# Shorter idle matmuls in the lead-in, and one unit's block sum rows written later: sparse attention followed by a gated feed-forward

## The chip, the core and the metric

The kernel runs on one core of one Trainium2 chip. The core has a matrix engine (TensorE, PE in the profile, with its weight loads as PEld), VectorE (DVE), ScalarE (ACT), GpSimd (POOL) and a queue engine, SyncE (SP), that here only issues transfers. Transfers are issued from two queues: GpSimd's (they cast from 32 to 16 bits on the way) and SyncE's. Sixteen DMA engines carry both. The metric is the device time of one execution in microseconds; lower is better.

## The reference

The input q, k, v are of shape (4, 8, 768, 64): four units of the batch, eight heads, 768 tokens, 64 numbers. A query sees the keys within 15 tokens of its own, and one summary for each block of 32 tokens (the maximum of its keys, the mean of its values). Then a feed-forward with a gate follows on all 3072 tokens.

```python
k_sum = k.reshape(B, H, nb, block, D).max(axis=3)      # block = 32, nb = 24
v_sum = v.reshape(B, H, nb, block, D).mean(axis=3)
scores_l = scale * np.matmul(q, k.transpose(0, 1, 3, 2))
mask_l = np.abs(pos[:, None] - pos[None, :]) < window   # window = 16
scores_s = scale * np.einsum('bhsd,bhnd->bhsn', q, k_sum) + np.log(block)
...
a = softmax of [scores_l where mask_l, scores_s]
attn = np.matmul(a, np.concatenate([v, v_sum], axis=2))
...
h = x @ w_in                                            # 512 -> 2048
g = h * (1.0 / (1.0 + np.exp(-1.702 * h)))
out = g @ w_out                                         # 2048 -> 512
```

## The kernel before

The four units run one after the other, and each in two halves of 384 tokens. While TensorE computes the feed-forward of one half, the attention of the next is spread between its products. Nearly all engine instructions go through one recording helper (`_Ordered`), which keeps them in the order of the program text on each engine; so all have line 28 in the profile, and tiles tell them apart.

**Lead-in (lines 870 to 980).** The first half of the first unit (the code's unit 0; the change's short description calls the half that follows it "unit 1") is computed on its own, as its data come in. GpSimd issues, in this order: k of the first unit (`load_k0`), q of its first half (`load_q0`), its v (`load_v0`), all of w_in in five parts (`load_w_in`), the first quarter of w_out, the "late q" (q of the second half, `load_q1`, three transfers of 128 tokens for all heads into `qb`), the other quarters of w_out, and then k, q and v of the next batch entry. TensorE has nothing to do until the first k lands; `idle` (line 283) gives it matmuls on a tile of zeros, `warm`, whose results nobody reads. They write the tile ps_h. The first block of them stands at line 902, ahead of the first k turn (`k_turn(0)`, transposes of kb into ps_k).

**The second half's values.** For the second half, `values` multiplies the exponentiated scores with rows of `vw[0]`, a tile in which each 64-query tile has its own 128 rows: 64 rows of v, then the halo of neighbouring v rows, then 24 block sums. Its own rows and the ones column are written by VectorE. The rest is the work of `vrows0` (line 317):

- four copies on VectorE from `vs4` (the sums, in four groups of partitions) to `vs` (32 rows);
- `halo_dmas`: four transfers on SP's queue within `vw[0]`, of 16 partitions each;
- `sum_dmas`: two transfers on SP's queue, 99 KB each, which write the rows of `vs` into `vw[0]`, once for each parity of the query tiles.

`vrows0` is called at line 994, right behind the two copies of v rows into `vw[0]`, while TensorE runs the first half's feed-forward input (`ff_in`, tiles `ph`). After it VectorE builds the second half's keys (tile `kx`). The tile `vs4` lies in the pool `lead`, which `early.close()` (line 1061) gives back; the tiles of the pool `snap`, above all `gs`, take its place in memory, and are first written in the next unit.

**The loop around the change (lines 1066 to 1072).** TensorE computes the first half's output product in twelve slots (`ff_out`, four products of 128x512 each into `po`), and `beside0` puts the second half's attention behind a slot, by this plan:

```python
plan0 = {1: ["q0", "q1", "q2"], 2: ["q3", "s0", "s1"], 4: ["s2", "s3"], 6: ["v0", "v1"], 8: ["x0"], 9: ["x1"]}
```

"q" is `q_late` (line 402): three transposes of the late q on TensorE into ps_q, then a copy on VectorE into qT. "s" is `scores` for one pair of heads (twelve products; exponent on ScalarE) and `mask` on VectorE; "v" is `values` for two pairs (the tile ps_av, 24 products each) and the division by their sums; "x" is the transposition of the result. The PSUM pool behind q0, q1, q3 and the scores has two buffers, taken in turn, so that the second score tile (s1) uses the bank that q3's copy reads. In the built program the first two weight loads and the second product of `v0` hold all the waits for the halo and row transfers.

Of the kernel before, what the change touches and what calls it, by code (L numbers as in the profile page):

```python
# [11 lines left out]
F16 = mybir.dt.float16  # L12
# [23 lines left out]
def kernel(  # L36
# [22 lines left out]
    NT = d_ff // 128  # L59
    HALF = S // 2  # L60
# [18 lines left out]
    early = ExitStack()  # L79
# [203 lines left out]
    def idle(n, cols=128):  # L283

        for i in range(n):
            pe.matmul(out=st["H", 0][:, 0:cols], lhsT=warm[:, 0:128], rhs=warm[:, 0:cols],
                      start=True, stop=True)
# [11 lines left out]
    def halo_dmas(w5, j0):  # L299
        halo_odd(w5, j0)  # L300
        halo_even(w5, j0)
# [10 lines left out]
    def sum_dmas(w5, j0, eng=sp):  # L312
        rows = vs[0:block].unsqueeze(1).to_broadcast([block, NJ - j0, H, VC])
        eng.dma_start(out=w5[64:64 + block, j0:NJ, 0], in_=rows)
        eng.dma_start(out=w5[0:block, j0:NJ, 1], in_=rows)

    def vrows0():

        v6 = vs4.rearrange("p (a g) c -> p g a c", g=4)
        o6 = vs.rearrange("p (a g) c -> p g a c", g=4)  # L320
        for g in range(4):
            dve.tensor_copy(out=o6[0:nb, g, :, 0:D], in_=v6[32 * g:32 * g + nb, g, :, 0:D])
        w5 = vw[0].rearrange("p (j e) h c -> p j e h c", e=2)
        halo_dmas(w5, JH)
        sum_dmas(w5, JH)
# [39 lines left out]
    def k_turn(p):  # L365
        ps = st["K", p] = pturn.tile([128, 1024], BF16, name="ps_k", tag="turn")
        o = 2 * (p % 2)
        for e in range(2):
            turn_plain(ps[:, e * HALF:e * HALF + HALF], kb2[p // 2][:, o:o + 2, e])
# [32 lines left out]
    def q_late(p, eng):  # L402
        if p != 2:
            ps = psb.tile([128, 2048], BF16, name="ps_q", tag="big")
        else:
            ps = pmm.tile([128, 1024], BF16, name="ps_q", tag="mm")
        turn_tiles(ps, qb2["late"][:, :, p], JH)
        copy(eng, qT[p][0][:, HALF:S], ps[:, 0:HALF])
# [163 lines left out]
    def scores(b, half, p):  # L572
        a = a_sb[half, p] = attp.tile([128, 2, TH, QT], BF16, name="a_sb", tag="a_sb")
        big = psb.tile([128, 1024], F32, name="ps_s", tag="big")
        score_tiles(big, p, b % 2, half)
        act.activation(out=a.rearrange("p h t c -> p h (t c)"),
                       in_=big.rearrange("p (h c) -> p h c", h=2)[:, :, 0:HALF],
                       func=ACT.Exp, scale=scale)

    def mask(half, p):  # L580
        a = a_sb[half, p]
        dve.tensor_mul(a, a, mk[:, half * TH:(half + 1) * TH, :].unsqueeze(1)
                       .to_broadcast([128, 2, TH, QT]))

    def values(b, half, g):

        if b == 1:
            banks = [pmm.tile([128, 512], F32, name="ps_av", tag="mm") for i in range(2)]
        else:
            ps = psb.tile([128, 1024], F32, name="ps_av", tag="big")  # L590
            banks = [ps[:, i * 512:i * 512 + 512] for i in range(2)]
        pvs = []
        for i in range(2):
            p = 2 * g + i
            a = a_sb[half, p]
            pv = banks[i][:, 0:390].rearrange("p (h j c) -> p h j c", h=2, j=JH)
            pvs.append(pv)
            for hh in range(2):
                for j in range(JH):
                    for e in range(2):  # L600
                        t = 2 * j + e
                        pe.matmul(out=pv[e * 64:e * 64 + 64, hh, j, :], lhsT=a[:, hh, t, :],
                                  rhs=vw[b % 2][:, half * TH + t, p + hh * NP if b else 2 * p + hh, 0:D + 1],
                                  start=True, stop=True, skip_group_check=True)
        x2[g] = attp.tile([128, 2, JH, 2, D], F16, name="x2", tag="x2", bufs=4)
        for i in range(2):
            norm(x2[g][:, :, :, i].rearrange("p h j d -> p j h d") if b else x2[g][:, i], pvs[i])
# [7 lines left out]
    def tx(half, g):  # L615
        ps = psb.tile([128, 2, HALF], F16, name="ps_x", tag="big")
        for i in range(2):
            for j in range(JH):
                pe.transpose(out=ps[:, i, j * 128:(j + 1) * 128],
                             in_=x2[g][:, i, j].rearrange("p h d -> p (h d)"), identity=ident16)  # L620
        dve.tensor_copy(out=xTT[half][g], in_=ps)
# [17 lines left out]
    def ff_in(half, nts):  # L639

        phs = [pmm.tile([128, HALF], F32, name="ph", tag="mm") for nt in nts]
        for part in ((0, 1), (2, 3)):
            for nt, ph in zip(nts, phs):
                ff_step(ph, half, nt, part)
        for nt, ph in zip(nts, phs):
            gelu(half, nt, ph)
# [31 lines left out]
    def w_sum(what, part):  # L678

        n = NT // 2  # L680
        c = slice(part * n // 2, (part + 1) * n // 2)
        w1, w2 = w_out_sb[:, 0:n], w_out_sb[:, n:]
        b11, b12, b21, b22 = w1[:, c, 0:N1], w1[:, c, N1:], w2[:, c, 0:N1], w2[:, c, N1:]
        a, b = {0: (b12, b11), 1: (b22, ws[:, 0, c]), 2: (b22, b12), 3: (b21, ws[:, 1, c])}[what]
        dve.tensor_tensor(out=ws[:, what, c], in0=a, in1=b, op=ALU.subtract)
# [161 lines left out]
    def ff_out(u, ms, part):  # L847
        if part == 0:
            po_now[ms] = pmm.tile([128, d_model], F32, name="po", tag="mm")
        po = po_now[ms]  # L850
        for nt in range(4 * part, 4 * part + 4):
            pe.matmul(out=po, lhsT=gT[u % 2][:, nt, ms * 128:(ms + 1) * 128],
                      rhs=w_out_sb[:, nt, :], start=(nt == 0), stop=(nt == NT - 1))
        if part == 3:
            osb = outp.tile([128, d_model], F32, name="osb", tag="osb")
            act.activation(out=osb, in_=po, func=ACT.Copy)
            r0 = u * HALF + ms * 128
            sp.dma_start(out=out[r0:r0 + 128, :], in_=osb)
# [5 lines left out]
    def gelu_soon():  # L864

        act.activation(out=gate[:, 1:2], in_=gate[:, 0:1], func=ACT.Gelu_apprx_sigmoid)
# [32 lines left out]
    dve.tensor_copy(out=ident16, in_=ident)  # L899

    st["H", 0] = pturn.tile([128, 512], F32, name="ps_h", tag="turn")
    idle(10, 512)
    k_turn(0)
    k_own(0, act)
    s_bias(0)
# [84 lines left out]
    for e in range(2):  # L990
        r = slice(64 * e, 64 * e + 64)
        dve.tensor_copy(out=w50[r, JH - e:NJ, e, :, 0:D],
                        in_=v0n[r, :, JH - e:NJ, 0:D].rearrange("p h j d -> p j h d"))
    vrows0()
    for s in range(2):
        clear_keys(dve, s)
    for p in range(NP):
# [18 lines left out]
    def beside0(slot):  # L1016
        for what in plan0.get(slot, ()):
            i = int(what[1])
            if what[0] == "q":
                q_late(i, dve)  # L1020
            elif what[0] == "s":
                scores(0, 1, i)
                mask(1, i)
                if i == NP - 1:
                    gelu_soon()
            elif what[0] == "v":
                values(0, 1, i)
            else:
                tx(1, i)
# [28 lines left out]

    for nt in range(N0, NT):
        ff_in(0, (nt,))  # L1060
    early.close()
    snap = ctx.enter_context(tc.tile_pool(name="snap", bufs=1))
    gs = snap.tile([128, 4, NT // 2, HALF], F16, name="gs")
    ws = keep.tile([128, 4, NT // 2, N1], F16, name="ws")
    exp_soon()
    beside0(-1)
    for i, (ms, part) in enumerate((ms, part) for part in range(4) for ms in range(JH)):
        ff_out(0, ms, part)
        beside0(i)
        if i in (10, 11):  # L1070
            w_sum(i - 10, 0)
            w_sum(i - 10, 1)
# [22 lines left out]
    for b in range(1, B - 1):  # L1095
# [32 lines left out]
        i = 0  # L1128
# [98 lines left out]
```

## Time and profile before

| | us |
|---|---|
| median of three timed runs | 209.07 |
| lowest, highest | 208.94, 209.77 |
| the profiled execution, its own time | 208.27 |
| its span, first to last instruction | 206.6 |

The profile shows one execution. The page's first part gives the busy time of each engine, in us and as a share of the span; VectorE is busy for 139.0 us, ScalarE for 123.5. The chain of waits goes back from the last instruction to what released it, step by step, so that the sum of its pieces is the span; pieces named PE are products, named DMA are transfers from issue to landing, "issue" is time in which the engine waited for nothing that the profile shows. In the timeline a row is a start, a length, an engine, the operation with its output and input tiles, and in brackets the idle time ahead of it with what ended it. An entry under SPq or POOL named DMA_DIRECT2D is the issue alone; when the data land is told by the view of a tile.

The page's second part, the span in 40 slices of 5.2 us, gives for TensorE

```profile
PE   7898997999999999999999999999999999999993
DMA  5999999999999999999999999995022940000222
```

where a digit is the busy share in tenths: TensorE has idle time in the first seven slices and the last one, and the DMA engines are occupied there from the second slice on, up to about 145 us.

### The profile page before, as it was taken

To read this page: it belongs to the slowest core of one execution; us is meant where nothing else is said; L and a number is where in the kernel's file an instruction comes from. 1 tells how busy PE (TensorE), PEld (TensorE's weight loads), DVE (VectorE), ACT (ScalarE), POOL (GpSimd) and SP (SyncE) were. 2 spreads that over 40 slices of the span, in tenths; PEclk is the share of its full clock that TensorE was granted. 3 is DMA by queue.
4 is the path that set the end of the run, shared out by engine and by line. 5 is a ranking of instruction groups with operands and counts; after the bars stand their busy time and mean duration, and the time that the engine had idled before them with its cause. 6 is when DMAs were issued, how large, how long until landed. Compare 5 with 4: busy or idle time off the path is not lost.

```text
span 206.6 us, 5777 instructions
## 1 busy us (share of the span) xinstructions
PE 198.3 (96%) x2326; PEld 135.6 (66%) x2326; DVE 139.0 (67%) x387; ACT 123.5 (60%) x236; POOL 93.7 (45%) x144
## 2 busy tenths in 40 slices
PE   7898997999999999999999999999999999999993
PEld 2566553466665566666788876566888865668882
DVE  4766892484965693899667779896769536758221
ACT  2374974637886736677773347778680567984220
POOL 7986588436899585000896017000000009991000
PEclk9999999999999999999999999999999999999999
DMA  5999999999999999999999999995022940000222
GB/s 57 154 159 201 203 197 211 197 157 210 153 148 136 182 174 162 113 172 153 118 160 183 198 115 138 189 223 126 3 105 57 175 127 0 3 0 0 105 102 103
DMA packets 99162, 27.73 MB, mean 134 GB/s; under 512 B 88752, under 2 KB 96192, under 8 KB 99136
## 3 DMA queue, kind: packets, MB, share of 16 engines
q0 software_dynamic: 73504, 13.64, 85.1%
q1 hardware_dynamic: 25632, 13.74, 33.2%
q8 instruction: 18, 0.29, 0.6%
q14 instruction: 8, 0.07, 0.1%
HBM read 27.26 MB, written 6.29 MB: 162 GB/s over the span
## 4 chain that ended last, share of the span: by engine, by line
PE 81%; DMA 12%; POOL 4%; issue 1%; DVE 0%; ACT 0%; POOLq 0%; DVEq 0%
PE ph L28 28%; PE poA L28 16%; PE po L28 10%; PE poB L28 8%; DMA qb<-in_q_dram 8%; DMA w_in_sb<-in_moe_w_in_dram 4%; PE poC L28 4%; PE phA L28 4%; PE ps_s L28 3%; PE ps_av L28 3%; POOL v0n L28 2%; POOL kb L28 1%; PE ps_t L28 1%; PE ps_x L28 1%; PE phB L28 1%; PE phC L28 1%
## 5 line engine op out<-in xcount | busy, mean ns | idle before, releaser
L28 PE MATMUL ph<-xT,w_in_sb 128*128 128x384 f16 x416 | 70.2, 326 | 0.1
L28 PEld LDWEIGHTS <-w_in_sb 128*128 128x128 f16 x452 | 43.7, 98 | 27.8 <-issue 0.2
L28 ACT ACTIVATE gT<-ph 128x384 f16<-128x384 f32 x104 | 49.8, 491 | 18.6 <-PE ph L28 18.3
L28 PEld LDWEIGHTS <-gT 128*128 128x128 f16 x312 | 28.9, 98 | 11.0
L28 ACT ACTIVATE a_sb<-ps_s 128x768 bf16<-128x768 f32 (+1 forms) x32 | 25.0, 826 | 13.8 <-PE ps_s L28 13.8
L28 PEld LDWEIGHTS <-gs 128*128 128x128 f16 x288 | 27.7, 98 | 3.4
L28 POOL DMA_DIRECT2D vw<-in_v_dram x36 | 24.6, 707 | 11.3 <-DMA kb<-in_k_dram 5.0
L28 POOL TENSOR_TENSOR gs<-gT 128x384 f16<-128x384 f16 x9 | 8.2, 910 | 42.4 <-ACT gT L28 42.4
L28 PE MATMUL po<-w_out_sb,gT 128*128 128x512 f16 x96 | 23.6, 380 | 0.0
L28 DVE TENSOR_TENSOR a_sb<-a_sb,mk 128x768 bf16<-128x768 bf16 x28 | 14.8, 554 | 6.5 <-ACT a_sb L28 5.9
L28 PE MATMUL poA<-ws,gs 128*128 128x256 f16 x144 | 18.7, 273 | 0.0
L28 DVE TENSOR_TENSOR x<-ps_av,rc 128x384 f16<-128x384 f32 x32 | 17.8, 557 | 1.1
L28 DVE TENSOR_TENSOR gs<-gT 128x384 f16<-128x384 f16 (+1 forms) x34 | 13.4, 393 | 7.2 <-ACT gT L28 6.9
L28 POOL DMA_DIRECT2D qb<-in_q_dram x17 | 16.4, 983 | 3.2 <-DMA v0n<-in_v_dram 1.1
L28 POOL DMA_DIRECT2D kb<-in_k_dram x16 | 15.3, 972 | 1.8 <-POOLq L1211 0.8
L28 PEld LDWEIGHTS <-kx 64*128 64x128 bf16 (+1 forms) x372 | 9.4, 95 | 6.6 <-issue 4.2
L28 DVE TENSOR_REDUCE ks<-kx 128x24 bf16<-128x768 bf16 x12 | 11.4, 948 | 3.4 <-ACT kx L28 3.2
L28 ACT ACT_TABLE_LOAD x10 | 12.8, 1283 | 1.0 <-PEq L1211 0.8
L28 ACT ACTIVATE osb<-poA 128x256 f32<-128x256 f32 x9 | 3.4, 383 | 15.8 <-PE poA L28 15.8
L28 ACT ACTIVATE s<-poA 128x256 f32<-128x256 f32 x11 | 4.2, 385 | 11.2 <-PE poA L28 11.2
L28 PEld LDWEIGHTS <-a_sb 128*64 128x64 bf16 (+2 forms) x400 | 7.9, 108 | 3.7 <-issue 2.2
L28 PE MATMUL poA<-w_out_sb,gT 128*128 128x256 f16 x72 | 9.4, 273 | 0.0
(112 smaller groups left out, 278.2 us busy)
## 6 DMA issues: line engine op xcount, KB each, us to landing
out_dram<-osb SPq DMA_DIRECT2D x23, 256.0 KB, 3.9
kb<-in_k_dram POOLq DMA_DIRECT2D x16, 192.0 KB, 6.3
qb<-in_q_dram POOLq DMA_DIRECT2D x14, 192.0 KB, 7.9
vw<-in_v_dram POOLq DMA_DIRECT2D x36, 64.0 KB, 5.4
w_out_sb<-in_moe_w_out_dram POOLq DMA_DIRECT2D x4, 512.0 KB, 16.3
w_in_sb<-in_moe_w_in_dram POOLq DMA_DIRECT2D x3, 512.0 KB, 12.6
vw<-vs SPq DMA_DIRECT2D x6, 198.0 KB, 5.6
v0n<-in_v_dram POOLq DMA_DIRECT2D x4, 192.0 KB, 7.8
```

The lines of the kernel that those rows point to most:

```text
L28: r = f(*a, **kw)
```

## The change

Three edits. The first idle block has 36 matmuls of 128 columns (the default of `idle`) instead of ten of 512. The call of `vrows0` moves from line 994 into the loop over the slots, behind `beside0(1)`: in program order that is after the copies of q0, q1 and q2 and before the copy of q3 on VectorE, and ahead of any later entry of SP's queue. And the end of the pool `lead`, with the two lines that open `snap` in its place, moves behind it, since `vrows0` reads `vs4`.

```diff
     st["H", 0] = pturn.tile([128, 512], F32, name="ps_h", tag="turn")
-    idle(10, 512)
+    idle(36)
     k_turn(0)
...
         dve.tensor_copy(out=w50[r, JH - e:NJ, e, :, 0:D],
                         in_=v0n[r, :, JH - e:NJ, 0:D].rearrange("p h j d -> p j h d"))
-    vrows0()
     for s in range(2):
         clear_keys(dve, s)
...
     for nt in range(N0, NT):
         ff_in(0, (nt,))
-    early.close()
-    snap = ctx.enter_context(tc.tile_pool(name="snap", bufs=1))
-    gs = snap.tile([128, 4, NT // 2, HALF], F16, name="gs")
     ws = keep.tile([128, 4, NT // 2, N1], F16, name="ws")
     exp_soon()
     beside0(-1)
     for i, (ms, part) in enumerate((ms, part) for part in range(4) for ms in range(JH)):
         ff_out(0, ms, part)
         beside0(i)
+        if i == 1:
+            vrows0()
+            early.close()
+            snap = ctx.enter_context(tc.tile_pool(name="snap", bufs=1))
+            gs = snap.tile([128, 4, NT // 2, HALF], F16, name="gs")
         if i in (10, 11):
             w_sum(i - 10, 0)
             w_sum(i - 10, 1)
```

In the built program SP's queue has the same order of transfers as before. The four halo transfers wait for the same VectorE instructions as before (the copies of v rows), the two transfers of `sum_dmas` for the copies into `vs` at their new place.

## The prediction

> **What bounds the kernel now.** I read the page's busy shares first, then the chain of waits in order of time, then the timeline of single engines around the two places that the change touches, and last the landing times of the transfers there.
>
> The page says that TensorE is busy nearly all the time, and the chain that the rest is its wait for transfers at the front:
>
> ```profile
> PE 198.3 (96%) x2326; PEld 135.6 (66%) x2326; DVE 139.0 (67%) x387; ACT 123.5 (60%) x236; POOL 93.7 (45%) x144
> PE 81%; DMA 12%; POOL 4%; issue 1%; DVE 0%; ACT 0%; POOLq 0%; DVEq 0%
> ```
>
> The chain in order of time (start, length in us, what):
>
> ```profile
> 10.29 8.47 DMA w_in_sb<-in_moe_w_in_dram
> 18.76 0.28 issue
> 19.04 15.70 DMA qb<-in_q_dram
> 34.74 0.05 issue
> 34.79 0.56 PE ps_q L28 x7
> ...
> 36.22 0.18 PE ps_q L28 x3
> 36.40 0.02 issue
> 36.43 0.37 DVE qT L28
> 36.79 0.04 issue
> 36.84 0.35 PE ps_s L28 x12
> ...
> 41.31 0.88 PE ps_av L28 x48
> 42.19 1.83 PE po L28 x8
> ```
>
> To be seen: until 34.74 us the end hangs on transfers, not on TensorE. The last third of the late q is issued at 19.04 and lands 15.70 us later. From 34.79 on the chain is TensorE itself almost without a gap, up to the last store. So what TensorE wins before 33.4 (its eight `po` products start at 31.46 and take 1.89) only lengthens its wait for q, and what it loses after 34.8 is lost at the end of the kernel too: no later piece of the chain is a transfer, so there is no cover.
>
> The two places of the change, in the timeline (start, length, engine):
>
> ```profile
> 1.30 3.96 PE L28 MATMUL ps_h<-warm 128*128 128x512 bf16 x10 [1.30 <-DVE warm L28]
> 4.26 0.15 PEld L28 LDWEIGHTS <-warm 128*128 128x128 bf16 x1 [0.28 <-issue]
> 4.67 0.10 PEld L28 LDWEIGHTS <-warm 128*128 128x128 bf16 x1 [0.26 <-issue]
> 5.20 0.36 PEld L28 LDWEIGHTS <-kb 128*64 128x64 bf16 x12 [0.42 <-DMA kb<-in_k_dram]
> 25.27 0.88 DVE L28 COPY vs<-vs 24x128 bf16<-24x128 bf16 x4
> 27.26 1.24 SPq L28 DMA_DIRECT2D vw<-vs  x2
> 35.13 0.89 DVE L28 COPY qT<-ps_q 128x384 bf16<-128x384 bf16 x3 [3.40 <-PE ps_q L28]
> 36.43 0.36 DVE L28 COPY qT<-ps_q 128x384 bf16<-128x384 bf16 x1 [0.41 <-PE ps_q L28]
> 41.24 0.95 PE L28 MATMUL ps_av<-vw,a_sb 128*64 128x65 bf16 x48
> ```
>
> And the view of the tile `vs`, for the two row transfers issued at 27.26 and 27.86:
>
> ```profile
> DMA to landing us min/median/max: 6.7/6.8/6.9
> ```
>
> So the rows landed at about 34.2 and 34.6, and the products that read them (`values`, ps_av) started at 41.24: nearly seven microseconds in hand. The change spends that reserve.
>
> **The lead-in.** Ten matmuls of 512 columns go, 36 of 128 come. The long ones started 0.425 us apart (their weight loads stand at 2.13, 2.56, 2.98), twice the 0.217 of a `po` product of the same 512 columns later (0.87 for four): the clock is still at half. It comes free between 4.26 and 4.67, where the weight load drops from 0.15 to 0.10. A short one costs a quarter, 0.106, until then: (4.65 − 1.30) / 0.106 = 31.6 of them; the other 4.4 at 0.057 (six transposes in 0.34) take 0.25, so the block ends near 5.0, where the long one ended at 5.26. The first k turn waits for its transfer until 5.20 in any case. If the weight load were not hidden, 36 × (0.15 + 0.106) = 9.2 us would be the price; the eight short idle matmuls at 8.80 take 0.62 in all, so it is hidden, and I take 0, ends −0.1 and +0.3. The cover is TensorE's wait for q, 1.4 us between 33.4 and 34.79.
>
> The row on the clock stands above: free 3.35 us after the first matmul. The Trainium skill (TensorE: Matmul & The Clock Gate, Part 1: The HAM clock gate) says that the warm-up is about 3.4 us of time and not a number of matmuls, in a window that runs free of the kernel's start. By that rule, too, short matmuls warm it alike, and the sum stays.
>
> **What leaves its old place.** Four copies on DVE (25.27, 0.88 us) and two transfers on SP's queue (27.26, 27.86). The four halo transfers ahead of them are issued at 24.54 to 26.65 and wait only for the `vw` copies: they stay. DVE's gain of 0.88 there is worth nothing, it waits 3.40 us for the late q anyway. The transfers' leaving is worth something: the q loads are moving at that time through the same engines. The rows are 2 × 99 KB; from 28 to 34 all queues together moved 202 GB/s on average, so 198 KB are 0.98 us; by packet time SP's queue held 26.8% of 6 us of the sixteen engines for 0.39 MB, half of it rows, 0.82 us. I take 0.8 (ends 0 and 0.98): q lands at 33.94, still after TensorE is free at 33.4, and the late q's three copies end at 36.02 − 0.80 = 35.22.
>
> **What comes in the new place.** On DVE the four copies stand between the third and the fourth of the late q's copies. The fourth is then late by 36.02 + 0.88 − 36.43 = 0.47 us, and behind it waits the second score tile (36.84, which starts when that copy ends, because it takes over the bank): TensorE loses 0.47. With q's gain TensorE would reach `values` at 41.31 − 0.80 + 0.47 = 40.98.
>
> But the rows are now late. Copies end: 35.22 + 0.88 = 36.10. SP's queue is empty then (its next entry, an output store, is at 45.88), so it issues 0.04 later, at 36.14 and, at 0.60 each, 36.74. How long the second takes to land is not in the trace for this place; the nearest rows:
> - the same two transfers now: 6.7 and 6.9, with the halos ahead of them in their queue;
> - a halo of 49.5 KB issued at 24.54 into an empty queue: 6.0;
> - output stores of 256 KB from 45.88 on, beside the k and v loads: 5.5, 6.0, 6.0;
> - the next batch entry's rows at 61.81, with GpSimd's queue almost drained: 4.7 and 5.4;
> - the last stores, with nothing else moving: 1.9.
>
> From 36 to 44 GpSimd's queue is full (205 GB/s to 40 us, then 156 to 170), as from 24 to 34. So the first three rows count; I take 6.6, ends 4.7 and 6.9. The rows have landed at 36.74 + 6.6 = 43.34, `values` starts 0.05 later at 43.39 (q's landing to its first use took 0.05). Both row transfers are waited for by the first two of its 48 products. Before, the chain has it at 41.31: **+2.1 us**. The 0.47 is inside this wait, and q's gain of 0.8 counts once, by moving the row's issue forward. Behind the waiting product stand all other products of TensorE in order, and with them everything to the end.
>
> **Sum.** The profiled execution took 208.27 (span 206.6 and 1.7 around it): 208.27 + 2.1 = 210.4. It is 0.8 under the median of the timed runs, 209.07, so for the median I say 209.07 + 2.1 = **211.2 us**. In general the start of `values` is 37.59 − (gain of q) + (landing time): with 5.5 to 6.9 and gains of 0.98 to 0.4 it is 42.1 to 44.1, which is +0.8 to +2.8, so 209.9 to 211.9 for this case alone.
>
> **Rivals.**
> - *The rows land in time (not slower).* If the second row transfer needs under 40.98 − 0.05 − 36.74 = 4.2 us, `values` doesn't wait, and what is left is −0.80 + 0.47 = −0.3: 208.7. For it: 1.9 with empty queues, 4.7 at 61.81; the rows would be alone in SP's queue. Against it: no transfer of SP's took under 5.5 while GpSimd's queue was full. Even with q's full 0.98 the gain is 0.5, so a gain of 0.5% of the time has almost no way. Chance 0.13.
> - The Trainium skill (DMA: Bandwidth & Descriptors, Anatomy of one DMA) fits a transfer by about 2.0 us and its bytes at 436 GB/s, there for GpSimd's path; worked out from this, as an estimate, 99 KB need 2.2 us, and this rival would hold. The trace's 5.5 to 6.9 under load disagree.
> - *q gains nothing.* If the late q is held by GpSimd's own packets and the rows only filled gaps, the gain is 0 and the landing still 6.6: `values` at 44.19, +2.9, 211.9. For it: packet times of both queues overlap (144.9% for GpSimd's from 28 to 34). Against: the moved bytes stay near 202 GB/s whichever queue moves them. Chance 0.10.
> - *The clock stays at half after the lead-in,* if short matmuls leave gaps. TensorE's work from 5.2 to 8.1, some 3 us, would double; its waits for transfers on the way (0.29, 0.18, 0.49) and the 0.6 left of its wait for q take about 1.6; 1.4 comes on top of 2.1: 212.6. Chance 0.04.
> - *The change doesn't do what it says:* `vrows0` also issues the four halo transfers, and if they moved with the call, their 181 KB would stand ahead of the rows behind the same late copies: four more issues of 0.6, so 2.4 more, 213.6. Against it: in the built program SP's order is unchanged and the halos wait for the same DVE instructions as before. Chance 0.02.
>
> **Chances.** The forecast has 0.71. About 0.5%, 1.05 us, is what a measurement of this kernel can tell from no change. Of the forecast's span the part below +1.05 is some 0.1; with most of the first rival that makes 0.21 for no difference; 0.02 for faster, 0.77 for slower. The range from 209.2 (landing in 5 us with q's full gain) to 212.3 (6.9 and a gain of almost nothing) leaves out the first rival and the dearest cases.
>
> **What would show it.** In the changed kernel's profile: q's last part landing near 33.9 and ps_q there; the `vs` copies between the third and fourth qT copy, near 35.2; the row transfers at about 36.1 with 6 to 7 us to land; a gap of about 2.4 us on TensorE before ps_av, put down to the transfer vw<-vs; the first k turn still near 5.2. I am wrong if ps_av follows its `po` products without a gap, or if the gap is there and a later wait of the chain has shrunk by as much.

## The result, and the profile after

| | before | changed |
|---|---|---|
| median, us | 209.16 | 215.50 |
| lowest to highest of four runs | 208.94 to 209.77 | 213.62 to 216.18 |
| profiled execution: time, span | 208.27, 206.6 | 213.62, 211.9 |

The changed kernel is slower: ratio 1.0284, 95% interval 1.0216 to 1.0352, which is 6.3 us in the medians. Ratios leave out executions over 1.5% above the fastest of their kernel. The sign was forecast; 2.1 us were forecast for the size, and the range ended at 212.3. The profiled execution, the fastest of the four, is 5.3 us longer than that of before (208.27, which is not among the four).

The chain of the changed kernel by engine, and in order of time around the late q (start, length in us, what):

```profile
PE 72%; DMA 18%; POOL 4%; DVE 2%; issue 1%; SPq 0%; ACT 0%; POOLq 0%; DVEq 0%
```

```profile
19.20 14.39 DMA qb<-in_q_dram
33.60 0.05 issue
33.64 0.24 PE ps_q L28
...
33.98 0.89 DVE qT L28 x3
34.87 0.10 DVE vs L28
34.97 0.01 issue
34.98 0.18 DVE vs L28
35.16 0.01 issue
35.18 0.80 DVE vs L28
...
36.83 7.58 DMA vw<-vs
44.41 0.14 issue
44.55 0.92 PE ps_av L28 x46
```

To be seen: q's last part lands at 33.59, 1.15 earlier than before. Behind it the chain leaves TensorE: the three copies of q, the four copies into `vs` (one of which took 0.80 us, not 0.19), the issue, and 7.58 us until the second row transfer has landed. The values start at 44.55 where they started at 41.31: **3.24 us** later, by the wait that was forecast, with 2.1.

The chain has a second wait of the same kind, in the next batch entry:

```profile
62.97 0.56 PE ps_vs L28 x48
...
65.09 0.59 SPq L28
65.68 0.05 issue
65.73 8.50 DMA vw<-vs
74.22 0.14 issue
74.36 0.54 PE ps_av L28 x23
```

These are the rows of the next entry's block sums, written by `value_rows(1)`, which the change doesn't touch; they are two transfers of 198 KB, twice the size of the moved ones. Before, they landed 4.7 and 5.4 us after issue and nobody waited; here are the view of `vs` there and the chain of before at its values:

```profile
DMA to landing us min/median/max: 4.7/5.0/5.4
```

```profile
68.08 0.97 PE po L28 x4
69.05 0.50 PE ps_av L28 x24
```

So its values started at 69.05, 27.74 after those of the second half of the first unit. Now they start 29.81 after them: **2.07 us** more. From there on the two chains have the same steps with the same lengths; 3.24 + 2.07 = 5.31 is the whole difference of the spans.

What GpSimd issues beside the rows is a likely reason; the experiments e3 and e4 test it. GpSimd's issues of the k loads for the entry after that, SP's of the rows, in the timeline of before and of the changed kernel:

```profile
61.24 4.04 POOL L28 DMA_DIRECT2D kb<-in_k_dram  x4
61.81 1.24 SPq L28 DMA_DIRECT2D vw<-vs  x2
```

```profile
62.47 4.04 POOL L28 DMA_DIRECT2D kb<-in_k_dram  x4
65.09 1.92 SPq L28 DMA_DIRECT2D vw<-vs  x2
```

The rows come 3.28 later, as TensorE does (their sums come from its products ps_vs). The k loads come only 1.23 later: before, GpSimd worked without a pause from 54.96 us on and was behind with its work, and TensorE's wait let it catch up (in the changed kernel it even waits twice, 0.18 and 0.24 us, just ahead of these loads). So the k loads lead the rows by 2.62 us, where it was 0.57.

The third part is not in the profiled execution but in the timed ones. Each run lists the mean clock that TensorE was granted: 1.000 for the profiled 213.62, and 0.992, 0.984 and 0.984 for 216.18, 215.40 and 215.59. In the changed kernel TensorE stands nearly still for 3.5 us (window of time; its length; busy time and number of instructions of PE, PEld, DVE, ACT and POOL; clock; DMA share; GB/s):

```profile
41.00:44.50 3.50, 0.19 (x1) 0.11 (x1) 0.10 (x1) 1.01 (x2) 1.20 (x2) 1.00 2.31 170
```

### The profile page after: what moved, and what is told of

It is laid out like the page before. It is cut to its first block, busy times and chain, and to the rows that moved or that the text cites. A ratio compares the mean times of both kernels' runs of the same rounds, so it can differ in the third digit from the quotient of the medians.

```text
span 211.9 us, 5828 instructions
## 1 busy us (share of the span) xinstructions
PE 198.6 (94%) x2352; PEld 138.4 (65%) x2352; DVE 139.4 (66%) x387; ACT 123.7 (58%) x236; POOL 95.0 (45%) x144
## 4 chain that ended last, share of the span: by engine, by line
PE 72%; DMA 18%; POOL 4%; DVE 2%; issue 1%; SPq 0%; ACT 0%; POOLq 0%; DVEq 0%
PE ph L28 27%; PE poA L28 15%; DMA vw<-vs 8%; PE poB L28 8%; DMA qb<-in_q_dram 7%; PE po L28 4%; DMA w_in_sb<-in_moe_w_in_dram 4%; PE poC L28 4%; PE phA L28 4%; PE ps_av L28 3%; PE ps_s L28 2%; POOL v0n L28 2%; POOL kb L28 1%; DVE vs L28 1%; PE ps_t L28 1%
## 5 line engine op out<-in xcount | busy, mean ns | idle before, releaser
L28 ACT ACTIVATE a_sb<-ps_s 128x768 bf16<-128x768 f32 (+1 forms) x32 | 25.1, 826 | 16.6 <-PE ps_s L28 16.6
L28 DVE TENSOR_TENSOR a_sb<-a_sb,mk 128x768 bf16<-128x768 bf16 x28 | 14.9, 554 | 6.5 <-ACT a_sb L28 5.9
L28 POOL DMA_DIRECT2D kb<-in_k_dram x16 | 15.3, 972 | 1.1 <-POOLq L1212 0.8
L28 ACT ACTIVATE osb<-poA 128x256 f32<-128x256 f32 x9 | 3.5, 384 | 15.8 <-PE poA L28 15.8
L28 PE MATMUL ps_av<-vw,a_sb 128*64 128x65 bf16 x336 | 7.4, 196 | 5.2 <-DMA vw<-vs 5.2
L28 DVE RECIPROCAL rc<-ps_av 128x6 f32<-128x6 f32 x32 | 6.0, 188 | 8.3 <-PE ps_av L28 8.0
## 6 DMA issues: line engine op xcount, KB each, us to landing
w_out_sb<-in_moe_w_out_dram POOLq DMA_DIRECT2D x4, 512.0 KB, 15.3
```

What stands on the lines that cost most here:

```text
L28: r = f(*a, **kw)
```

## The experiments

Four sets, each on one chip beside the kernel before (medians there 209.14, 209.15, 208.63 and 209.35).

**The idle matmuls alone (e1).** `idle(36)` in the kernel before, nothing else.

> Kernel before with the 36 short idle matmuls in place of the ten long ones, the row transfers left where they were. Theory (the whole loss is the rows' late landing and what follows from it): first k turn within 0.1 us of 5.20, median within 0.4 us of before, 209.1. Rival (the short idle matmuls leave the clock at half for longer, or move the front): 1 us or more slower, TensorE's products behind 5 us still at half speed.

208.84, ratio 0.9991 (0.9967 to 1.0015); the first k turn at 5.10. The idle matmuls have no part in the loss.

**The move alone (e2, and e11 beside the changed kernel, e10).** The change without `idle(36)`.

> Kernel before with the move of the row writing alone, the ten long idle matmuls kept. Theory: the same as the changed kernel, 213.6 to 216.2; the second row transfer lands 7 to 8 us after issue, ps_av starts near 44.5, a second wait of about 2 us stands before the next batch entry's first values. Rival (the idle matmuls have a part of the loss): 2 us or more below the changed kernel.

> The changed kernel again, beside the move alone on one chip. Theory (the idle matmuls have no part): the same median as the move alone within 0.7 us. Rival (short idle matmuls leave TensorE's clock in a worse state further on): 1 us or more above the move alone.

> The move alone (ten long idle matmuls) beside the changed kernel on one chip. Theory: same as the changed kernel within 0.7 us. Rival: 1 us or more below it.

e2: 213.37, ratio 1.0207 (1.0164 to 1.0249), inside what the rival of 2 us or more below the changed kernel foresaw. But the changed kernel had been timed on another chip. Side by side e10 has 216.12, ratio 1.0269 (1.0225 to 1.0313), and e11 215.50, ratio 1.0286 (1.0237 to 1.0335): no difference. The move is the whole of it.

**TensorE late for another reason (e3).** The kernel before with 58 dummy products ahead of the second half's values (`values`, where the batch entry is 0 and g is 0):

```diff
+            if b == 0 and g == 0:
+                for i in range(58):
+                    pe.matmul(out=ps[:, 0:128], lhsT=ident, rhs=ident, start=True, stop=True,
+                              skip_group_check=True)
```

> Kernel before, rows written in the old place, with 58 dummy matmuls of 128 columns on TensorE (0.057 us each, 3.3 us) ahead of the second half's first values, where the changed kernel waits. Theory (the second wait, of 2.1 us at the next batch entry's first values, comes from TensorE being late against GpSimd's queue, whatever made it late): 3.3 + 2.1 = 5.4 slower, about 214.5, with the second wait of 1.5 to 2.5 us on the transfer vw<-vs. Rival (the second wait belongs to the moved transfers themselves): 3.3 slower, 212.4, no wait there. No half clock in either, since TensorE works all the time.

212.39, ratio 1.0163 (1.014 to 1.0186). The chain of e3:

```profile
64.86 0.58 SPq L28
65.45 0.05 issue
65.50 7.37 DMA vw<-vs
72.87 0.14 issue
73.00 0.54 PE ps_av L28 x23
```

The second wait is there, with the moved rows in their old place: the k loads led the rows by 2.62 us (62.24 and 64.86), as in the changed kernel, the rows landed in 7.4 us and not 5.4, and TensorE waited 0.76 us for them. So a late TensorE is enough for it. But it is less than the 1.5 to 2.5 that I expected, and the median has only 3.25 more, the matmuls alone. What gave the rest back in the timed runs is open.

**The k loads held (e4).** The changed kernel, with one line in `load_batch`:

```diff
+        if b == 2:
+            pool.tensor_copy(out=gate2[0:32], in_=vs[0:32, 0, 0:1])
```

> Changed kernel, with one added GpSimd copy that reads the next batch entry's block sums before GpSimd issues the k loads of the entry after that; so these loads are issued no earlier than the row transfers, as they nearly were in the kernel before. Theory (those k loads, issued 2.6 us ahead of the rows, hold the rows up): the rows land in 4.7 to 5.5 us, not 7.6 and 8.5, the second wait is gone, 2.1 us faster than the changed kernel (211.5 where the clock is full, 213.4 median). Rival (the loads don't matter): no difference.

The k loads at 65.78, the rows at 66.17, landed in 4.7 and 6.2. The chain goes through the place without a transfer:

```profile
72.14 0.28 PE ps_s L28 x12
72.42 0.97 PE po L28 x4
73.39 0.50 PE ps_av L28 x24
```

So with GpSimd's loads held back, the second wait is gone. The added copy holds back all that GpSimd issues behind it, so that the k loads and the v loads after them are not told apart. The other profiles mostly say the same of the slower of the two row transfers: where the k loads led by 2.3 to 2.7 us it took 7.4 to 9.2 us (nine profiles), where they led by 0.2 to 0.6 it took 5.4 to 6.7 (before, e1, e4, e7, e13). The exception is e12: a lead of 0.40, 8.1 us, and a wait of 1.45. So the lead is not the only thing that makes these rows late. The median, 212.96 with a ratio of 1.0194 (1.016 to 1.0228), can't be set against 215.5 from another chip; against e2 beside it, it is 0.4 less, not the 2.1 that I expected. By the profiles, e2's second wait was only 1.07 us, and e4's first values started later than e2's (44.06 against 43.62). All four runs of e4 have a clock of 0.991 or 0.992, and its profile shows where:

```profile
36.00:40.60 4.60, 4.42 (x52) 2.04 (x51) 2.17 (x5) 2.74 (x5) 1.70 (x2) 1.00 1.43 204
40.60:44.10 3.50, 0.28 (x5) 0.17 (x6) 0.20 (x1) 1.11 (x2) 1.21 (x2) 1.00 2.28 168
44.10:47.50 3.40, 3.40 (x52) 2.02 (x53) 2.45 (x8) 0.00 (x0) 1.51 (x3) 0.50 2.64 154
47.50:51.00 3.50, 3.50 (x26) 1.94 (x25) 1.90 (x4) 0.80 (x2) 1.85 (x3) 1.00 2.29 134
```

The columns are those of the window above; the one ahead of the DMA share is the clock. TensorE does next to nothing for 3.5 us, and then its clock is at half for 3.4 us: the 47 products of ps_av take 1.47 us there, where 46 took 0.92 at full clock in the changed kernel.

A shorter pause was enough in other runs. In e2, e11 (both above) and e9 (below) TensorE stood for 2.6, 2.3 and 2.3 us ahead of the same products (with 0.19 us of work in it), and its clock was at half for 3.4 us from 44.4, 44.2 and 43.3 on. The timeline of e9:

```profile
41.66 0.19 PE L28 MATMUL ps_av<-vw,a_sb 128*64 128x65 bf16 x1 [0.49 <-DMA vw<-vs]
43.43 1.50 PE L28 MATMUL ps_av<-vw,a_sb 128*64 128x65 bf16 x47 [1.58 <-DMA vw<-vs]
```

**The wait filled (e5, e6).** The changed kernel again, and beside it the changed kernel with 48 such dummy products ahead of the values.

> The changed kernel once more, to stand beside the next run on one chip. Theory (the timed runs lie above the profiled 213.6 because TensorE stands for 3.5 us before ps_av and its clock then falls to half for 3.4 us, once or twice): most runs with a mean clock of 0.984 to 0.993, these slower by 1 to 2.5 us than a run with 0.998 or more. Rival (the spread has nothing to do with the clock): no such order.

> The changed kernel with 48 dummy matmuls of 128 columns (2.7 us) on TensorE in the first wait, just ahead of the second half's first values. Theory: the wait ends when it did (landing of the second row transfer, near 44.4), but the clock stays full after it: the half-clock stretch behind 44 us is gone, and the median is 1 to 2 us below the changed kernel on the same chip. Rival: the same median, or 2.7 more if the matmuls come on top of the wait.

| | us, and mean clock, of six runs |
|---|---|
| e5 | 213.72 (0.989), 214.85 (0.992), 215.12 (0.989), 215.76 (0.984), 218.17 (0.976), 219.06 (0.969) |
| e6 | 212.24 (1.000), 212.46 (0.999), 212.67 (1.000), 212.99 (0.997), 213.54 (0.999), 214.28 (0.990) |

Ratios to before 1.0257 (1.0204 to 1.0311) and 1.017 (1.0125 to 1.0215), which are 1.8 us apart; the medians of all six, 215.44 and 212.83, are 2.6 apart. All but one of the runs of e6 lie below every run of e5. No run of e5 had a clock near 1, so that the order that I expected within e5 can't be seen; five of six of e6 have 0.997 or more. In e5's profile (the run of 219.06) the clock is at half from 17.2 to 20.7, from 44.6 to 51.4 behind the first wait and from 78.7 to 82.1 behind the second. More matmuls, about 1.8 us less: the wait ends when the transfer lands in either, and the half clock behind it is gone:

```profile
42.00:46.00 4.00, 2.72 (x48) 2.53 (x45) 0.03 (x1) 0.94 (x2) 1.68 (x3) 1.00 2.39 165
46.00:49.40 3.40, 3.39 (x64) 2.18 (x65) 2.67 (x9) 0.00 (x0) 1.71 (x3) 1.00 2.85 148
```

e6's 214.28 with its 0.990 is the profiled run; its half clock lies in the lead-in, not here.

**Both helps (e13).** The dummy products and the held k loads in the changed kernel.

> Changed kernel with both helps: the 48 dummy matmuls in the first wait and the GpSimd copy that holds the next k loads until the next sums stand. Theory (the loss is three terms: the first wait of 3.2, the second of 1 to 2, the half clock of 1 to 2.5): only the first wait is left, 3.0 to 3.6 over before, clock 0.997 or more in most runs, second row transfer at 66 us landing in 5 to 6.2 us and no wait behind it. Rival (a further term): 4.5 or more over before.

212.62, ratio 1.0141 (1.0087 to 1.0195), 3.3 over before. In its profile: k loads at 64.10, rows at 64.50, landed in 4.6 and 6.1; values at 43.93 and 71.71, so 27.78 apart, as before the change. Four of six runs have 0.998 or more. No fourth term is left to be found in the median; the interval is wide, 1.8 to 4.1 us.

**What makes the moved rows land late (e9, e14).** The changed kernel with `load_batch(1)` called behind `vrows0`; in e9 GpSimd first reads `vs`, in e14 the landed rows in `vw[0]`.

```diff
     clear_values(dve, 1)
-    load_batch(1)
...
             vrows0()
+            pool.tensor_copy(out=gate2[0:32], in_=vw[0][0:32, 2 * JH + 1, 0, 0:1])
+            load_batch(1)
```

> Changed kernel with GpSimd's loads of the next batch entry (k, q, v) held until the sums stand in vs, so that the row transfers at 36.2 us meet only the last two quarters of w_out on the DMA engines. Theory (what makes the second row transfer land 6.6 to 8.5 us after issue is the queue of GpSimd's loads: w_out until 39 us holds up its first packet by some 4 us, the small packets of k behind it spread the rest): it lands 4 to 5.5 us after issue, ps_av starts 2 to 3 us sooner than in the changed kernel, near 42. Rival (the landing time belongs to the transfer itself, 32 partitions with repeated rows): 6.6 us or more all the same. The late loads may cost time further on; the median is no test.

> Changed kernel with GpSimd's k, q and v loads of the next batch entry held until the moved rows have landed, so that no small packet of k meets them. Theory (the w_out queue holds the first packet back for 2 to 4 us and the small k packets stretch the rest): second row transfer lands 3.5 to 4.8 us after issue, ps_av near 41.5. Rival (the landing time is the transfer's own): 6 us or more. The late loads cost time further on; the median is no test.

e9: 5.1 and 6.3 us; its k loads went out at 36.29, with the rows. e11, with the k loads in their early place, has 6.3 too, so e9 tells nothing. e14, the view of `vs` around 36 us and the timeline of TensorE:

```profile
DMA to landing us min/median/max: 5.2/5.3/5.5
```

```profile
41.45 0.92 PE L28 MATMUL ps_av<-vw,a_sb 128*64 128x65 bf16 x47 [0.74 <-DMA vw<-vs]
```

With no k packet about, 5.5 us and not 7.6, which is less than in any other run with the rows in this place and more than the 3.5 to 4.8 that I expected. The k loads are part of the landing time; most of it stays without them. The copies into `vs` took 0.77 us in e14 and 1.39 in the changed kernel, where GpSimd issued a q load at the same time (34.91, 1.05 us long) and one copy took 0.80. The held loads cost time further on (213.68 in the median of e9, 213.75 in that of e14, two runs each).

**The rows elsewhere (e7, e8, e12).** e7: `vrows0` behind VectorE's work on the keys, ahead of the late q's copies. e8: in the old place, the two row transfers replaced by two copies on VectorE. e12: e8 with the held k loads.

> Kernel before with the row writing called later, but earlier than in the change: behind all of VectorE's work for the second half's keys and ahead of the late q's copies (about 32 us). Theory (the gain for q is real, 0.8 to 1.1 us, and what costs is only the landing after TensorE needs the rows): q's last part lands near 33.7, the rows near 39.5, ps_av follows without a wait, 0.5 to 1.1 us below before. Rival 1 (q gains nothing): as before. Rival 2 (rows issued later land later than 41 in any place): slower than before by up to 1 us.

> Kernel before with the two row transfers replaced by two copies of 32 partitions on VectorE in the same place; no transfer writes these rows. Theory: q lands 0.8 to 1.1 us earlier as in the changed kernel, VectorE's added 1 to 2 us lie in its 3.4 us of waiting for q, no wait at ps_av: 0.5 to 1.1 us below before. Rival (the row transfers didn't hold q up, it landed earlier by chance): as before.

> Kernel before with the rows written by two VectorE copies in the old place, and the added GpSimd copy that holds the next k loads until the next entry's sums stand. Theory (both waits on row transfers have no more cause): 0.5 to 1.2 us below before. Rival (in most runs TensorE itself is late at the late q, so that an earlier q gives nothing, and before has no second wait): as before.

| | median, us | ratio to before |
|---|---|---|
| e7 | 208.91 | 0.9990 (0.9963 to 1.0017) |
| e8 | 208.70 | 0.9970 (0.9938 to 1.0002) |
| e12 | 208.92 | 1.0002 (0.9975 to 1.0030) |

e7's rows went out at 33.66, landed in 5.5, and its values followed without a wait. None of the three is told from before. In e7's profile TensorE itself came late to the late q (clock at half from 16.6 to 20.0), and found it landed; there an earlier q is worth nothing. How many of the timed runs are like this one is open, and so is whether e8 gains a few tenths. The profiles of e8 and e12, each the longest execution of its kernel, have the second wait too (1.65 and 1.45 us), with no moved rows to wait for. In e8 the k loads went out 1.65 earlier than before (59.59) and led the rows by 2.33; in e12, where they were held, what made the rows late is open. No version beat the kernel before.

## Why the prediction went wrong

- **The lead-in at 0: right.** The short block ended at 5.32, the first k turn was at 5.25; e1 shows no difference.
- **q's gain, 0.8: 1.15 in the profile,** and the late q's three copies ended at 34.87 (35.22 forecast). The other profiles bear it out: the last third of the late q took 15.6 to 15.8 us to land with the rows in the old place (before, e1, e3), 14.3 to 14.8 in most runs without them there, 15.2 in e9 and 15.3 in e7. That it is paid out at the end was not shown: e8, which keeps the gain without the first wait (14.5), and e7, which keeps a third of it, are not told from before.
- **Four copies, 0.88: 1.39.** I took the duration from a place where GpSimd wasn't issuing a transfer. The issue of the rows came out at 36.20 and 36.83 all the same (36.14 and 36.74 forecast), for q was earlier.
- **Landing in 6.6: 7.58,** and 6.3 to 8.5 over the profiles of the changed kernel and its variants with the k loads in their early place. My upper end, 6.9, was the same transfers at 27 us, where the packets beside them were those of the late q and w_out. At 40 us they are the next entry's k, and with these held back (e14) the landing took 5.5. The 4.7 and 5.4 in my list were for transfers of 198 KB, a size that the list left out. With an issue 0.09 later and 0.14 from landing to first use, where I had 0.05, this is 3.24 and not 2.1.
- **The step that failed:** "Behind the waiting product stand all other products of TensorE in order, and with them everything to the end." I carried the wait to the end as a shift of everything, and had said that no later piece of the chain was a transfer, so that there was no cover. Both treat the other engines as if they moved with TensorE. GpSimd, which had been behind with its work, moved its loads by only 1.23 when TensorE moved by 3.28, so that a transfer with reserve before came into the chain: 2.07 us (e3 shows it with TensorE delayed by other means, though smaller; e4 takes it away; e12 has such a wait without the lead, so that the lead is not the whole cause). The profile of before had its warning: rows landing at 67.9 for values at 69.05, a reserve of 1.2 us.
- **A term that was missing:** the clock. My rival with the half clock looked at the lead-in alone, and for the clock behind the wait I put nothing, without a reason. A wait of the size that I forecast, about 2.4 us, was enough for it: 2.3 us in the profiles of e9 and e11. Filling the wait was worth 1.8 us by the ratios of e5 and e6.
- **The rivals:** rows in time, which I gave 0.13, did not come in any profile with the row transfers in the new place. That q gains nothing is out: it gained 1.15. The half clock in the lead-in cost nothing in e1. The low end of my range doesn't follow from its own terms: 37.59 − 0.98 + 5 is +0.3, so 209.4 and not 209.2. The halo transfers stayed where they were, at 23.99 to 26.94. The rule of thumb that I cited from the Trainium skill (DMA: Bandwidth & Descriptors, Anatomy of one DMA), 2.2 us as an estimate for 99 KB, is far from the 5.1 to 8.5 of the moved transfers in these runs.

The Trainium skill (TensorE: Matmul & The Clock Gate, Part 1: The HAM clock gate) has the clock fall back after at least one idle window of about 3.4 us, in windows that run free of the kernel. These runs agree on the length and on the windows: each half-clock stretch or half of a double one lasts 3.41 us, and in one run they start whole multiples of 3.41 us apart (17.60, 44.91 and 79.04 in e10's profile, 8 and 10 of them). They differ on the idle window: in the 3.41 us ahead of a fall TensorE had been busy for 0.24 us in e4, but for 1.03 in e2, 1.27 in e11, 1.46 in e9, and for 1.8 to 2.3 in the lead-in of e1, e5, e6, e7, e8, e10 and e12. So a window need not be idle, and a pause shorter than 3.4 us is not safe. Nor does a long one always bring it: the first profile has 1.000 with a pause of 3.5 us.

## To carry to other kernels

A wait put into the bounding engine is not a rigid shift: ask which queues don't move with that engine, what they will now have issued ahead of its next transfers, and how much reserve those transfers had. A transfer's landing time is a property of the place more than of its size: here 99 KB took 5.1 to 8.5 us at the place of the change, and 198 KB in the next batch entry 3.6 to 9.2; the long times went mostly with what another queue had issued in the two or three microseconds before. And a pause of TensorE of 2.3 us or more can have a second price, which the fastest execution doesn't show; look at the clock of every run, not only at the one profile.

## What the runs showed of the hardware

- The half-clock stretches of 3.4 us also come in the lead-in, from 11 us on: in e1's profile (11.5 to 14.9) they cost nothing that shows, 208.60 being under the median, because TensorE then waits for q anyway. Later ones do show: in e5, e6, e7, e8 and e10, with the half clock between 16.6 and 21.0, TensorE came to the late q only at 34.2 to 35.1 and found it landed, where the changed kernel started on it at 33.64.
- 48 dummy products, 2.8 us of added work, made a kernel 1.8 us faster by the ratios to before (e6 against e5).
- A VectorE copy of 24 partitions, 0.19 us elsewhere, took 0.80 while GpSimd issued a transfer, in the changed kernel, e4, e11 and e13; in e14, where GpSimd held still, none did. The Trainium skill (SBUF — State Buffer, Terms) says that the two share a port pair that one holds for a whole instruction while the other stands; the runs fit this, but no run was made to test it.
